# Issuing one small store of the output from SyncE instead of GpSimd, at the end of a gated attention and convolution kernel

## The chip, the cores and the metric

One core of a Trainium2 chip. The kernel is one program with an instruction stream for each engine: TensorE (PE, matmuls), VectorE (DVE), ScalarE (ACT), GpSimd (POOL) and SyncE (SP). DMAs are started by instructions in the streams of SP, ACT and POOL and are carried out by the core's 16 DMA engines. The metric is the device time of one execution in microseconds (us), median of several runs.

## The reference

Two branches over a sequence of 2048 rows and 448 columns, mixed by a gate for each row:

```python
def reference(A_x, A_wq, A_wk, A_wv, A_wo, B_u, B_A_re, ..., B_log_dt, B_Dskip, gate_w):
    def _A_ref(x, wq, wk, wv, wo):        # attention: 16 heads of 28, one key and value head
        q = (x @ wq).reshape(B, S, H, Dh).transpose(0, 2, 1, 3)
        k = x @ wk
        v = x @ wv
        scores = jnp.einsum("bhqd,bkd->bhqk", q, k) * (Dh ** -0.5)
        p = _softmax(scores, axis=-1)
        o = jnp.einsum("bhqk,bkd->bhqd", p, v)
        return o.transpose(0, 2, 1, 3).reshape(B, S, H * Dh) @ wo
    def _B_ref(u, A_re, A_im, B_re, B_im, C_re, C_im, log_dt, Dskip):
...
        P = jnp.exp(logdA[:, :, None] * l[None, None, :])
        K = jnp.einsum("dn,dnl,dn->dl", Cc, P, dB).real      # one filter of 2048 taps for each column
...
        return y + u * Dskip[None, None, :]                  # y: each column of u convolved with its filter
    g = _sigmoid((x * gate_w).sum(-1, keepdims=True))
    return g * a + (1 - g) * b
```

Inputs and output are bf16; the output has 1 x 2048 x 448 elements.

## The kernel before

**The output in SBUF.** The tile `O` has 128 partitions and 16 blocks of 448 columns. Partition p of block t holds row 1024 * (p // 64) + 64 * t + p % 64, so one block is 64 rows of the first half of the sequence and 64 of the second. A store from `O` to the output is therefore always a pair of DMAs, one for each half (`rows`, L1272).

**Who writes `O`.** The convolution goes by chunks of 16 columns, 28 of them (`conv`, 0 to 27): matmuls (L1155) of filter against input, a multiplication by 1 - g (L1170, tile `cst`), a transposition on PE (L1181), and an addition into `O` on DVE (L1189), which touches the chunk's 16 columns in all 16 blocks. So the last 32 columns of every block are complete only with chunks 26 and 27, the last two. The attention branch goes by query blocks; for each block of rows the output projection (L1198, and L1265 for the last one) is multiplied by the gate and added into `O` on DVE (`fold`, L1207). The two kinds of additions commute, and the kernel keeps two keys for each part of the rows: `O` for columns 0 to 415, and `Oz` for the last 32.

**How the output leaves.** All in `tail` (L1250):

- `out0` to `out3` (L1276): columns 0 to 415 of blocks 0 to 14, four pairs of DMAs on SP, which need `O` alone.
- `outz0` and `outz1` (L1282): the last 32 columns, pieces of 64 bytes. `outz0` holds blocks 0 to 7 (m = 8, 512 pieces for each of the two DMAs), `outz1` blocks 8 to 14 (m = 7, 448 pieces for each). Each needs the additions of chunks 26 and 27, and those of the attention for its rows. `outz0` is issued by POOL, `outz1` by ACT.
- `outl0` and `outl1` (L1285): block 15 with all its columns, one DMA each, 64 pieces of 896 bytes, issued by SP and by ACT.

The `outz` and `outl` stores wait for the addition of chunk 27 (L1189), the `out` stores do not.

**What sets the order.** The kernel builds a list of operations with their dependences (`op`, `dma`) and a planner (`schedule`, L178) sets the order on each engine. It simulates the engines: of all operations that are ready it takes the one with the smallest key (time at which it can start, priority `pr`, place in the list), over all engines, and puts it at the end of its engine's stream. The stores all have priority 1. `emit` (L400) then writes each engine's stream in that order, each operation with its waits on semaphores; a DMA adds 16 to the semaphore of its name when it has landed. A stream runs in order: an operation that waits holds up all behind it on its engine. At the end of its stream SP waits for all semaphores whose names begin with `out` (L430 and L431).

**The end of the program.** The streams stand in a block (`with nc.Block() as block`, L483). When its stream ends, each engine drains, and then the engines wait for each other on two semaphores; POOL collects the arrivals and lets the others go. In the profile these instructions carry line 483.

Of the kernel before, what the change touches and what calls it, by code (L numbers as in the profile page):

```python
# [75 lines left out]
def dram(t, off, dims):  # L76
    return bass.AP(tensor=t.tensor, offset=t.offset + off, ap=[list(d) for d in dims])
# [381 lines left out]
class Kernel:  # L459
# [790 lines left out]
    def tail(self):  # L1250
        pg = self.pg
        self.norm_last(14, 0, 512, None, [("on", 2)])
        self.norm_last(15, 0, 256, None, [("on", 3)])
        for tt in range(2):
            self.outp(3, tt)
        self.norm_last(15, 256, 128, None, [("on", 4)])
        self.outp(3, 2)
        self.evac(15, 384, 128)
        self.norm_last(15, 384, 128, 1, [("on", 5)])
        t, o = self.bank(2)  # L1260
        px = lambda: t.v(0, P, o, [[1, D]])
        X, key = ("ox", 3, 3), [("b", 2)]
        on = [("on", 0), ("on", 1), ("on", 2), ("on", 5)]
        for g in range(4):
            pg.op("pe", lambda e, g=g: e.matmul(  # L1265
                px(), self.onT.v(0, P, g * 512 + 384, [[1, 128]]), self.Wo.v(0, P, g * D, [[1, D]]),
                start=(g == 0), stop=(g == 3), tile_position=(0, 0), skip_group_check=True), 200,
                rd=["Wo", on[g]], wr=[X] + key, pr=1 if g < 3 else 0.5)
        self.fold(3, 3, px, 0, D, [X])
        D0 = D - 32  # L1270
        n0 = len(pg.ops)
        rows = lambda t0, m, d0, n: [(dram(self.out, (1024 * h + 64 * t0) * D + d0, [[D, 64], [64 * D, m], [1, n]]),  # L1272
                                      self.O.v(64 * h, 64, D * t0 + d0, [[D, m], [1, n]])) for h in range(2)]
        for qc in range(4):
            m = 4 if qc < 3 else 3
            pg.dma(rows(4 * qc, m, 0, D0),  # L1276
                   (128 * m, 832), f"out{qc}", rd=[("O", q) for q in ([qc], range(3, 6))[qc == 3]], pr=1)
        for i in range(n0, len(pg.ops)):
            pg.after[i] = self.lastT
        for k, e in enumerate(("pool", "act")):  # L1280
            m = 8 - k
            pg.dma(rows(8 * k, m, D0, 32),  # L1282
                   (128 * m, 64), f"outz{k}", rd=[("Oz", q) for q in (range(2), range(2, 6))[k]], pr=1, eng=e)
        for h, e in enumerate(("sp", "act")):
            pg.dma(rows(15, 1, 0, D)[h:h + 1], (64, 896), f"outl{h}", rd=[("O", 6), ("Oz", 6)], pr=1, eng=e)  # L1285
# [193 lines left out]
```

## Time and profile before

| | |
|---|---|
| median of 3 runs | 511.47 us (511.31 to 512.3) |
| the profiled execution | 510.55 us |
| its span in the profile | 508.8 us |
| mean granted TensorE clock | 0.978 |
| busy: PE, DVE, ACT, POOL | 429.2, 454.5, 481.6, 167.0 us |
| last exponential on ACT ends | 493.85 us |
| last addition into `O` on DVE ends | 499.34 us |
| stores of the output issued | 475.9 to 501.5 us |

Times in the profile are counted from the start of its span, in us; the span begins with the first instruction of the program and ends with its last, and the time of an execution is a little longer. A name like L1189 is a line of the kernel. An engine's name with a q (POOLq, SPq) stands for its instruction stream: DMA issues on SP and ACT, waits, drains. A line such as "A <- B" in a list of waits says that A stood idle until B was done; where several things were waited for, the one that came last by the profile is named. The chain is followed backwards from the last busy instruction, and issuing a DMA on POOL counts as busy, while drains and semaphores do not.

In the 40 slices of the span, ACT is 90% busy or more from the fifth slice to the 36th; the last slice, from 496.1 us on, holds the last matmuls, the last additions and the stores:

```profile
PE   6798778888888898889888899989888899998891
...
DVE  7999899999999999999999999999999999624152
ACT  5997999999999999999999999999999999998970
POOL 8632224152152510515422421535151324240001
```

### The profile page before, as it was taken

Reading aid. Unit: us, or ns where it says so; the run is one execution under the profiler, and the core shown is the slowest. Engines: PE = TensorE matmul, PEld = TensorE weight load, DVE = VectorE, ACT = ScalarE, POOL = GpSimd, SP = SyncE. Lnnn points to the kernel's source line nnn. Section 1 sums busy time; section 2 is a strip of 40 time slices with the busy share of each in tenths; the row PEclk is TensorE's granted clock in tenths of the full one; section 3 lists DMA queues with packets and bytes.
Section 4 is the critical chain, followed back from the end, with each engine's and each line's share of the span. In section 5 each row is a group of like instructions: output and inputs, shape, how many; then the busy total and the mean of one; then the engine's idle time right before and its main releaser. Section 6 shows DMA issues by size and latency. Waiting matters only on the chain.

```text
span 508.8 us, 18819 instructions
## 1 busy us (share of the span) xinstructions
PE 429.2 (84%) x8362; PEld 195.4 (38%) x8469; DVE 454.5 (89%) x834; ACT 481.6 (95%) x432; POOL 167.0 (33%) x310
## 2 busy tenths in 40 slices
PE   6798778888888898889888899989888899998891
PEld 2322223343334334344443344444433444344551
DVE  7999899999999999999999999999999999624152
ACT  5997999999999999999999999999999999998970
POOL 8632224152152510515422421535151324240001
PEclk8997999999999999999999999999999999998996
DMA  8979702989959897999999999599999989899932
GB/s 189 220 209 136 51 22 60 331 243 366 359 149 320 260 295 244 299 367 345 348 316 367 306 364 358 150 351 363 363 301 372 312 297 366 266 379 371 385 119 46
DMA packets 122404, 139.51 MB, mean 274 GB/s; under 512 B 55145, under 2 KB 62346, under 8 KB 122322
## 3 DMA queue, kind: packets, MB, share of 16 engines
q1 hardware_dynamic: 111152, 128.82, 79.3%
q0 software_dynamic: 8720, 9.31, 6.7%
q8 instruction: 66, 1.08, 0.9%
q10 hardware_dynamic: 2450, 0.17, 0.3%
q14 instruction: 16, 0.13, 0.1%
HBM read 125.18 MB, written 5.22 MB: 256 GB/s over the span
## 4 chain that ended last, share of the span: by engine, by line
ACT 52%; DVE 36%; PE 8%; issue 2%; DMA 1%; SPq 1%; POOL 0%
ACT expT L1357 52%; DVE tab L1048 4%; DVE tab L1060 3%; DVE tab L1059 3%; DVE msq L991 2%; DVE tab L1070 2%; DVE tab L1058 2%; DVE tab L1057 2%; DVE mbf L1011 2%; PE psS L1332 1%; DVE T L888 1%; DVE seedz L995 1%; PE psB L1383 1%; DVE seedz L993 1%; DVE tmp L1066 1%
## 5 line engine op out<-in xcount | busy, mean ns | idle before, releaser
L1357 ACT ACTIVATE expT<-psS 128x1536 bf16<-128x1536 f32 (+1 forms) x410 | 465.4, 1336 | 6.4 <-PE psS L1323 3.5
L1332 PE MATMUL psS<-qM,kT 128*128 128x512 bf16 (+2 forms) x369 | 104.0, 357 | 28.4 <-ACT expT L1357 14.5
L1383 PE MATMUL psB<-expT,vaug 128*32 128x512 bf16 (+2 forms) x1152 | 102.9, 367 | 2.5 <-issue 1.1
L1323 PE MATMUL psS<-qT,kT 29*128 29x512 bf16 (+2 forms) x699 | 82.4, 363 | 23.4 <-ACT expT L1357 21.5
L154 POOL DMA_DIRECT2D KP_scratch<-kstg x112 | 61.0, 553 | 66.3 <-DVE kstg L1110 37.9
L1048 DVE TENSOR_TENSOR tab<-tab,mbf 128x512 bf16<-128x512 bf16 (+3 forms) x56 | 64.5, 1153 | 0.0
L1383 PEld LDWEIGHTS psB<-expT,vaug 128*32 128x32 bf16 x1152 | 27.5, 93 | 75.4 <-issue 70.4
L154 POOL DMA_DIRECT2D rdenB<-R_scratch x56 | 28.9, 522 | 60.7 <-DMA R_scratch<-denT 51.9
L1332 PEld LDWEIGHTS psS<-qM,kT 128*128 128x128 bf16 x455 | 28.6, 98 | 48.7 <-ACT expT L1357 33.4
L1323 PEld LDWEIGHTS psS<-qT,kT 29*128 29x128 bf16 x699 | 21.3, 91 | 67.3 <-ACT expT L1357 55.7
L154 POOL DMA_DIRECT2D qM<-qT x64 | 32.2, 511 | 35.4 <-DVE qT L966 20.0
L1060 DVE TENSOR_TENSOR tab<-tab 128x128 bf16<-128x128 bf16 (+4 forms) x70 | 41.5, 594 | 0.0
L1059 DVE TENSOR_TENSOR tab<-tab 128x1024 bf16<-128x1024 bf16 (+4 forms) x70 | 41.4, 593 | 0.0
L1155 PE MATMUL psS<-T,U 128*32 128x128 bf16 (+3 forms) x1504 | 35.7, 222 | 0.5 <-DVE qT L966 0.4
L154 POOL DMA_DIRECT2D denT<-acc x14 | 10.0, 715 | 75.5 <-DVE kstg L1106 37.3
L1070 DVE TENSOR_TENSOR tab<-tab,tmp 128x4096 bf16<-128x4096 bf16 x14 | 32.0, 2287 | 0.1
L1058 DVE TENSOR_TENSOR tab<-tab,mbf 128x4096 bf16<-128x4096 bf16 x14 | 31.9, 2279 | 0.0
L1057 DVE TENSOR_TENSOR tab<-tab,mbf 128x4096 bf16<-128x4096 bf16 x14 | 31.9, 2278 | 0.0
L1155 PEld LDWEIGHTS psS<-T,U 128*32 128x32 bf16 (+3 forms) x1504 | 25.3, 95 | 14.2 <-issue 9.9
L1155 PE MATMUL psX<-T,U 128*32 128x128 bf16 (+7 forms) x1216 | 28.8, 220 | 0.4 <-issue 0.2
L991 DVE TENSOR_TENSOR msq<-seedz 128x384 f32<-128x384 f32 (+1 forms) x50 | 27.0, 540 | 0.2
L1066 DVE TENSOR_TENSOR tmp<-tmp,mq 128x64 bf16<-128x64 bf16 (+4 forms) x70 | 25.4, 362 | 0.1
(161 smaller groups left out, 536.8 us busy)
## 6 DMA issues: line engine op xcount, KB each, us to landing
T<-KP_scratch SPq DMA_DIRECT2D x170, 512.0 KB, 9.4
U<-KP_scratch SPq DMA_DIRECT2D x40, 512.0 KB, 10.0
tab<-KP_scratch SPq DMA_DIRECT2D x14, 512.0 KB, 10.6
rdenB<-R_scratch POOLq DMA_DIRECT2D x56, 64.0 KB, 5.5
qM<-qT POOLq DMA_DIRECT2D x64, 32.0 KB, 5.2
tab<-in_A_x_dram SPq DMA_DIRECT2D x8, 224.0 KB, 3.6
O<-cst SPq DMA_DIRECT2D x1, 1792.0 KB, 11.5
KP_scratch<-kstg POOLq DMA_DIRECT2D x112, 16.0 KB, 4.1
```

What stands on the lines that cost most here:

```text
L154: return [e.dma_start(o, i, **kw) for o, i in pairs]
L1048: vo(lambda e, dst=dst, src=src, mri=mri: e.tensor_tensor(dst, src, mri, ALU.mult), 4 * n, done + mk(lv), [kr, ki, tk])
L1057: vo(lambda e, src=src, mi=mi, tv=tv: e.tensor_tensor(tv, src, mi, ALU.mult), 2 * n, done + mk(lv), [tk])
L1058: vo(lambda e, dst=dst, src=src, mr=mr: e.tensor_tensor(dst, src, mr, ALU.mult), 2 * n, done + mk(lv), [kr, ki, ("gap", s)])
L1059: vo(lambda e, dc=dc, tc=tc: e.tensor_tensor(dc[0], dc[0], tc[1], ALU.subtract), n, [tk, kr], [kr])
L1060: vo(lambda e, dc=dc, tc=tc: e.tensor_tensor(dc[1], dc[1], tc[0], ALU.add), n, [tk, ki], [ki])
L1070: vo(lambda e: e.tensor_tensor(tab.v(0, P, FM, [[4, 1024], [1, 4]]), tab.v(0, P, lo + 124, [[CG, 32], [-4, 32], [1, 4]]), rho.v(0, P, 0, [ ...
L1155: r = e.matmul(ps.v(32 * j, 32 - 2 * n, 128 * k, [[1, 128]]), self.U.v(0, P, (4 * gi + j) * 32 + 2 * n, [[1, 32 - 2 * n]]), tbuf.v(0, P, t ...
L1323: r = e.matmul(self.psS.v(0, P, 512 * b + o, [[1, n]]), kT.v(32 * h, DH + 1, 128 * kt, [[1, 128]]), qT.v(32 * h, DH + 1, 512 * (i % 2) + q ...
L1332: r = e.matmul(self.psS.v(0, P, 512 * b + o, [[1, n]]), kT.v(0, P, 128 * kt, [[1, 128]]), self.qM.v(0, P, (i % 2) * XQ + 512 * h + qo, [[1 ...
L1357: pg.op("act", lambda e: e.activation(expT.v(0, P, 512 * es[0], spread(es, n)), self.psS.v(0, P, 512 * bs[0], spread(bs, n)), AF.Exp, scal ...
L1383: r = e.matmul(self.psB.v(32 * h, 32, qo, [[1, n]]), vaug.v(0, P, 32 * kt, [[1, 32]]), expT.v(0, P, 512 * ring[t] + o, [[1, n]]), start=(k ...
```

## The change

The engine of `outz0` is SyncE instead of GpSimd. Its two DMAs, their addresses and sizes, what they depend on, their priority and their place in the list stay. `outz1` stays on ACT.

```diff
--- before.py
+++ after.py
@@ -1277,7 +1277,7 @@
                    (128 * m, 832), f"out{qc}", rd=[("O", q) for q in ([qc], range(3, 6))[qc == 3]], pr=1)
         for i in range(n0, len(pg.ops)):
             pg.after[i] = self.lastT
-        for k, e in enumerate(("pool", "act")):
+        for k, e in enumerate(("sp", "act")):
             m = 8 - k
             pg.dma(rows(8 * k, m, D0, 32),
                    (128 * m, 64), f"outz{k}", rd=[("Oz", q) for q in (range(2), range(2, 6))[k]], pr=1, eng=e)
```

## The prediction

> **What bounds the kernel now.** I read the page first (span, slices, chain shares), then the chain in order of time for the last 14 us, then the end of the program, line 483, then the stores one by one.
>
> ```profile
> span 508.8 us, 18819 instructions
> ...
> ACT 52%; DVE 36%; PE 8%; issue 2%; DMA 1%; SPq 1%; POOL 0%
> ```
>
> Until 493.85 us the last exponential on ACT ends the chain (its timeline row: 487.39 + 6.46), and nothing of that stretch is touched. The chain in order of time shows what follows; columns are start, duration, what.
>
> ```profile
> 497.59 0.69 DVE cst L1170
> ...
> 498.91 0.43 DVE O L1189
> 499.34 0.28 issue
> 499.62 1.44 POOL out_dram L154 x2
> ```
>
> DVE's last addition into O, of convolution 27, ends at 499.34. It releases every store that holds the last 32 columns. The chain ends with POOL's second issue at 499.62 + 1.44 = 501.06, but the span ends at 508.8: 7.7 us have no busy instruction at all. What stands there is seen at line 483, the end of the program's block, where each engine drains and then meets the others (columns: durations in ns, minimum/median/maximum, then first and last start in us):
>
> ```profile
> L483 POOLq EVENT_SEMAPHORE  x2: 17/17/17, 508.6 to 508.7; - x2
> ...
> L483 DVEq DRAIN  x1: 441/441/441, 498.9 to 498.9; - x1
> L483 POOLq DRAIN  x1: 8215/8215/8215, 500.4 to 500.4; - x1
> L483 ACTq DRAIN  x1: 401/401/401, 501.6 to 501.6; - x1
> ...
> L483 SPq DRAIN  x1: 13/13/13, 503.9 to 503.9; - x1
> L483 SPq EVENT_SEMAPHORE  x1: 17/17/17, 508.7 to 508.7; - x1
> ```
>
> Read it by who comes last. PE, DVE and ACT are drained by 502.0. SP, which waits for all stores, is drained at 503.9. POOL's drain starts at 500.4, lasts 8.215 us and ends at 508.6, and only then do the event semaphores of all engines pass, 0.2 us before the span ends. The waits of SP's queue say the same from the other side: 3.7 us for the stores to land, then 4.8 us at line 483 (the engine named there, PE, was long done; POOL's drain is the one still open).
>
> ```profile
> SPq L483 <- PEq L483: 4.8, 1, 4.8
> SPq L431 <- DMA out_dram<-O: 3.7, 2, 3.5
> ```
>
> So the end is set by POOL's drain behind its last two DMAs, by 508.6 - 503.9 = 4.7 us over SP.
>
> **The change part by part.**
>
> Removed from POOL: two DMA issues. POOL's timeline shows what is then its last work:
>
> ```profile
> 453.34 2.00 POOL L154 DMA_DIRECT2D rdenB<-R_scratch  x4 [1.08 <-DVE onT L1225]
> 499.62 1.44 POOL L154 DMA_DIRECT2D out_dram<-O  x2 [44.28 <-DVE O L1189]
> ```
>
> Its instructions end at 455.34, so its drain comes 44 us earlier. How long a drain is there the trace does not show; the bounds are the 183 ns of POOL's drain at line 1464, at the start, before any DMA of its own, and the 8.2 us above. I take 8.2, as it too stands behind POOL DMAs: it ends at about 463.5. Either costs nothing, since ACT works until 493.85, DVE until 499.34 and the stores until 503.7; it would count only from over 48 us on. With that cover gone it is the 4.7 us of today.
>
> Added to SP: the same two DMAs (512 pieces of 64 bytes each). SP has nothing between the rest of `out3` (issued from 495.88) and its `outl0` at 499.36, for which it waited 2.2 us on the same DVE addition. Both are ready at that point, of one priority, and `outz0` comes first in the list, so I expect `outz0`, `outz0`, `outl0`. SP is moved past nothing else: behind `outl0` stands only its wait for all stores. The trace has these rows for stores of the output (columns as above):
>
> ```profile
> L154 SPq DMA_DIRECT2D out_dram<-O x9: 493/1215/1538, 475.9 to 499.4; - x9
> L154 ACTq DMA_DIRECT2D out_dram<-O x3: 656/704/735, 499.4 to 500.9; - x3
> L154 POOL DMA_DIRECT2D out_dram<-O x2: 714/726/738, 499.6 to 500.4; - x2
> ```
>
> and among the DMA issues from 455 us on, with size and median us from issue to landing:
>
> ```profile
> out_dram<-O POOLq DMA_DIRECT2D x2, 32.0 KB, 3.0
> out_dram<-O SPq DMA_DIRECT2D x1, 56.0 KB, 1.9
> out_dram<-O ACTq DMA_DIRECT2D x2, 28.0 KB, 2.8
> out_dram<-O ACTq DMA_DIRECT2D x1, 56.0 KB, 2.8
> ```
>
> One issue of 512 small pieces on SP is not in the trace. Bounds: 0.49 us (SP's `outl0`) and 0.84 (ACT's 0.735 for 448 such pieces, times 8/7); I take 0.74, about ACT's longest, and with 0.03 us between issues, as ACT has. Then `outl0` is issued at 499.36 + 2 x 0.77 = 500.90 instead of 499.36. For its landing the bounds are 1.9 (its own now) and 3.2 (the slower of ACT's two 28 KB stores); I take 2.8, that of ACT's `outl1`, which like it stands third behind two small-piece stores. It lands at 503.7. ACT's `outl1`, untouched, is issued at 500.86 and also lands at 503.7, today's last landing. The 16 DMA engines have as much to move as before, and are no more than 0.62 busy in any stretch from 500 on (the windows by stage).
>
> The sum: last landing 503.7, as today; SP's last waits, branch and drain 0.25 behind it, as today (503.96 is the drain's end); release of the barrier 0.2, as between POOL's drain and the span's end, and 0.1 for SP's signal to reach POOL, an estimate from the less than 0.1 between the event semaphores there. 503.96 + 0.04 + 0.2 + 0.1 = 504.3 against 508.8, a gain of 4.5 us. The profiled execution took 510.55 with 1.75 outside the span, which I leave as it is, and lies 0.9 below the median of the runs; on that median 511.47 - 4.5 = **507.0 us**.
>
> Its own range: landing 2.3 (ACT's first small store) instead of 2.8, should POOL's packets no longer be in the way of either queue, gains 0.5 more; issues of 0.84 and a landing of 3.2 lose 0.6; the runs before spread over 1.0. That is 506.0 to 508.2.
>
> **The rivals.**
>
> One generator for both hardware queues. If SP's and ACT's issues could not overlap, six would follow each other from 499.36: 2 x 0.74, 0.704, 0.735, 0.656, 0.49 and gaps, 4.2 us together, so the last is issued near 502.95 and lands at 505.8, 2.1 later. Gain 2.4, **509.0 us**. For it: at 499.36, where SP and ACT issue at the same moment, ACT's issue took no less than its later ones, so nothing excludes a wait inside it. Against it: from 0.81 to 3.59 SP made four issues in 2.78 us, its usual 0.6 to 0.8 each, while ACT made its own from 0.81 on without a break. Chance 0.10. [...]
>
> The drain does not follow POOL's last DMA but the end of all work. Then it would outlast the last landing as now, by 4.9 us, and the time stays at **511.5 us**. For it: POOL's issues were done at 501.06 and its data had landed at 503.5, yet the drain ran 5.1 us longer, so it waits for something else than these. Against it: SP's and ACT's drains end without any such tail, and at 39.5 us a POOL copy starts right as the DMA before it ends, so DMAs leave nothing behind on POOL that every later step must wait for. Chance 0.13. That the store lands no sooner is granted already: the gain comes from the drain alone.
>
> The other side: SP is held up at its issue. SP's longest issue in this kernel is 5.56 us (one of the four loads of `Wo` from 33.2 on), where its queue had much in front. Should both small-piece stores be held so, `outl0` comes 2 x (5.56 - 0.74) = 9.6 us later, the end at 513.9, and the time is **516.6 us**, slower. It decides from the point where the two issues together take over 1.5 + 4.5 = 6.0 us. For it: `outz0` and `outl0` would share one queue, and SP's issues while its queue was full (475.9 to 483.3) took 1.2 to 1.5. Against it: `out3` has landed by then but for its last pieces, and ACT issues the same kind in 0.70 to 0.735. Chance 0.07.
>
> That the change does not do what it says comes to an order: with `outl0` ahead of `outz0`, the second `outz0` is issued at 500.66 and lands at 503.9 with the 3.2 of ACT's second, 507.2 us, inside the forecast's range.
>
> **How the numbers follow.** Forecast 0.70, shared generator 0.10, drain at the end 0.13, held-up SP 0.07. A difference under 0.2% (1.0 us) can hardly be told from none here. Faster: 0.70 + 0.10 = 0.80; within: 0.13; slower: 0.07. The range takes in the forecast's own and the shared generator with a little beside: 505.9 to 509.3; the two cases outside make 0.20.
>
> **What would show it.** In the changed kernel's line 483, POOL's drain starts near 455 and SP's is the last, near 504; SP's wait at line 483 falls from 4.8 to some tenths. Line 154 has three SP issues from 499.36 on, of 0.5 to 0.84 each, and no POOL store. Landings of `outl0` and `outl1` near 503.7. The prediction is wrong if POOL's drain still ends 4 us or more behind the last landing, if the SP issues overlap ACT's only in turn (over 1.4 us each), or if the exponentials end later than 493.9, which nothing here should move.

## The result and the profile after

The changed kernel takes 507.12 us (median of 6 runs, 505.02 to 507.33), the kernel before 511.39 (6 runs, 510.78 to 512.3): a ratio of 0.9909, 95% interval 0.989 to 0.9927, or 4.3 us less. In a later comparison it was 506.97 (5 runs) against 512.09 (11 runs), 0.9902, 0.9878 to 0.9926.

Line 483 of the changed kernel, the end of the program's block (durations in ns minimum/median/maximum, then first and last start in us):

```profile
L483 POOLq EVENT_SEMAPHORE  x2: 17/17/17, 504.8 to 505.2; - x2
L483 POOLq DRAIN  x1: 10101/10101/10101, 457.0 to 457.0; - x1
...
L483 DVEq DRAIN  x1: 441/441/441, 500.4 to 500.4; - x1
L483 ACTq DRAIN  x1: 404/404/404, 503.1 to 503.1; - x1
...
L483 SPq DRAIN  x1: 13/13/13, 504.8 to 504.8; - x1
```

POOL's drain now runs from 457.0 to 467.1, while ACT is still at its exponentials. SP is the last to drain, and POOL's event semaphores follow, at 504.8 and 505.2. The waits of SP's queue show the same: 4.8 us at line 483 have become 0.5, and the wait for the stores has fallen from 3.7 to 1.5, as SP is busy issuing from 500.86 to 502.81.

```profile
SPq L431 <- DMA out_dram<-O: 1.5, 2, 0.8
SPq L483 <- PEq L483: 0.5, 1, 0.5
```

The stores of the output (issues at line 154, and for those from the last addition on, size and us to landing):

```profile
L154 SPq DMA_DIRECT2D out_dram<-O x11: 596/637/1582, 478.4 to 502.2; - x11
L154 ACTq DMA_DIRECT2D out_dram<-O x3: 662/720/787, 500.9 to 502.4; - x3
```

```profile
out_dram<-O SPq DMA_DIRECT2D x2, 32.0 KB, 2.2
out_dram<-O ACTq DMA_DIRECT2D x2, 28.0 KB, 2.4
out_dram<-O SPq DMA_DIRECT2D x1, 56.0 KB, 2.1
out_dram<-O ACTq DMA_DIRECT2D x1, 56.0 KB, 2.1
```

The last piece of the chain in this profile is DVE's addition:

```profile
499.09 0.69 DVE cst L1170
499.78 0.60 DVE O L1207
500.38 0.02 issue
500.41 0.42 DVE O L1189
```

It stands 1.5 us later than before (500.83 against 499.34), so the spans, 505.3 and 508.8, differ by 3.5 only. I don't put that shift down to the change: a second profile of the same kernel has the last addition at 503.92, and eleven profiles of kernels whose streams are the same up to POOL's last load have the last exponential ending between 492.7 and 498.4. What the change touches is the stretch behind that addition. I call it the tail, and it repeats to hundredths: **9.48 us before, 4.45 and 4.46 in the two profiles after**. That is 5.0 us less; the medians give 4.3 to 5.1.

### The profile page after: what moved, and what is told of

It is laid out like the page before. It is cut to its first block, busy times and chain, and to the rows that moved or that the text cites. A ratio compares the mean times of both kernels' runs of the same rounds, so it can differ in the third digit from the quotient of the medians.

```text
span 505.3 us, 18926 instructions
## 1 busy us (share of the span) xinstructions
PE 448.2 (89%) x8469; PEld 195.1 (39%) x8469; DVE 455.0 (90%) x834; ACT 482.6 (96%) x432; POOL 165.3 (33%) x308
## 3 DMA queue, kind: packets, MB, share of 16 engines
q0 software_dynamic: 8656, 9.25, 6.7%
## 4 chain that ended last, share of the span: by engine, by line
ACT 48%; DVE 38%; PE 10%; issue 2%; DMA 1%; SPq 1%
ACT expT L1357 48%; DVE tab L1048 5%; DVE tab L1059 3%; DVE tab L1060 3%; DVE msq L991 3%; DVE tab L1070 2%; DVE tab L1058 2%; DVE tab L1057 2%; DVE mbf L1011 2%; PE psS L1332 2%; PE psB L1383 2%; DVE seedz L995 2%; PE psS L1323 2%; DVE seedz L993 1%; DVE tmp L1066 1%
## 5 line engine op out<-in xcount | busy, mean ns | idle before, releaser
L1332 PE MATMUL psS<-qM,kT 128*128 128x512 bf16 (+2 forms) x455 | 122.5, 360 | 13.8 <-ACT expT L1357 10.5
```

The costliest lines, as they stand in the source:

```text
L1332: r = e.matmul(self.psS.v(0, P, 512 * b + o, [[1, n]]), kT.v(0, P, 128 * kt, [[1, 128]]), self.qM.v(0, P, (i % 2) * XQ + 512 * h + qo, [[1 ...
```

## The experiments

All are the changed kernel with one edit, but for three small ones at the end. The table holds what the traces gave, in us behind the end of the last addition into `O` (negative: ahead of it). "POOL ends" is the end of POOL's last instruction ahead of its drain.

| kernel | POOL ends | POOL's drain ends | SP's drain ends | tail |
|---|---|---|---|---|
| before | 1.74 | 9.25 | 4.63 | 9.48 |
| after | -43.1 | -33.7 | 3.95 | 4.45 |
| after_again | -44.1 | -34.3 | 3.95 | 4.46 |
| tiny_end | 0.79 | 8.22 | 5.27 | 8.74 |
| memset_end | 0.17 | 7.54 | 3.95 | 8.06 |
| tiny_mid | -2.70 | 4.74 | 3.94 | 5.26 |
| tiny_early | -10.8 | -3.4 | 3.96 | 4.17 |
| memset_early | -11.4 | -4.1 | 3.96 | 4.18 |
| memset_461 | -37.6 | -30.3 | 3.97 | 4.19 |
| on_act | -44.3 | -34.5 | 5.58 | 6.09 |
| halves | -44.1 | -34.2 | 3.94 | 4.43 |

**A late DMA on POOL, but a tiny one.** All stores stay where the change put them; POOL gets one of 64 bytes to a scratch tensor `Z`.

```diff
+        pg.dma([(dram(self.Z, 0, [[32, 1], [1, 32]]), self.O.v(0, 1, 0 * D + D0, [[1, 32]]))], (1, 64), "outd", rd=[("Oz", q) for q in range(2)], pr=1, eng="pool")
```

> The changed kernel with one more DMA on POOL: a single 64-byte piece of O into a scratch tensor in DRAM, released by the same last addition as outz0, so that POOL again has a DMA at its very end, but a tiny one, while all stores of the output stay on SP and ACT. Theory drain (the gain is that POOL's drain of 8 to 10 us no longer stands behind a late DMA): the drain starts some 0.5 us behind the last addition into O and ends 8.8 to 10.5 us behind it; the tail from that addition to the end of the span goes from 4.45 back to 9 to 10.7 us, the time from 507.1 to about 511.6 to 513.3. Rival landing (the gain is that 64 KB land sooner through a hardware queue): tail 4.5 to 5.0, time 507.1 to 507.6. Rival size (the drain is long because 1024 pieces went through POOL): drain well under 4 us, time about 507.1.

Measured: 510.18 us (10 runs) against 511.35, ratio 0.9978, 0.9954 to 1.0002. The tail is 8.74. POOL's timeline and line 483 of this kernel:

```profile
499.97 0.50 POOL L154 DMA_DIRECT2D Z_scratch<-O  x1 [43.43 <-DVE O L1189]
```

```profile
L483 POOLq EVENT_SEMAPHORE  x2: 17/17/17, 508.2 to 508.3; - x2
...
L483 POOLq DRAIN  x1: 7952/7952/7952, 500.0 to 500.0; - x1
...
L483 SPq DRAIN  x1: 13/13/13, 504.9 to 504.9; - x1
```

POOL's drain is last again by 3 us. So it is not the 64 KB, nor where they land, that costs, and a drain behind 64 bytes is as long as one behind 1024 pieces: 7.43 us from the end of POOL's last instruction, 7.51 before. The sizes expected, a tail of 9 to 10.7 us and 511.6 to 513.3 us of time, were too high, since I had counted with the drain of 10.1 us at 457.

The tiny DMA did one thing more in this profile. The six stores behind the addition, issued as in the changed kernel, all took 1.3 to 1.7 us longer to land (that kernel's rows, above, have 2.2, 2.4, 2.1 and 2.1):

```profile
out_dram<-O SPq DMA_DIRECT2D x2, 32.0 KB, 3.7
out_dram<-O ACTq DMA_DIRECT2D x2, 28.0 KB, 4.0
out_dram<-O SPq DMA_DIRECT2D x1, 56.0 KB, 3.4
out_dram<-O ACTq DMA_DIRECT2D x1, 56.0 KB, 3.4
```

So the last landing is at 5.02 instead of 3.70, and SP's drain at 5.27. The tail doesn't feel it, as POOL's drain ends later still, at 8.22. The name `outd` makes SP wait for the tiny DMA too, but that landed at 501.63, before any of the six.

**The same DMA earlier.** It is released by the addition of block 12 (`rd=[("O", 3)]`), with columns of that block as its source.

> The same tiny DMA on POOL, released by the gated addition of block 12 into O instead (about 11.6 us ahead of the last addition). Theory drain: the drain starts there and is over 1.5 to 3 us ahead of the last addition, so the tail stays at 4.45 us and the time at 507.1, within 0.5. Rival that one more POOL DMA costs by itself, wherever it stands: tail 9 us, 511.6.

Measured: 506.24 us (4 runs) against 511.35, 0.9898, 0.9853 to 0.9943. The drain is as long, and hidden:

```profile
L483 POOLq DRAIN  x1: 7952/7952/7952, 487.8 to 487.8; - x1
...
L483 SPq DRAIN  x1: 13/13/13, 503.1 to 503.1; - x1
```

**No late DMA at all, only a late end of POOL's stream.**

```diff
+        pg.op("pool", lambda e: e.memset(self.denT.v(0, P, 0, [[1, 16]]), 0.0), 100, rd=[("Oz", q) for q in range(2)], wr=["dn"], pr=1)
```

> The changed kernel with a small memset on POOL (16 columns of denT, not used afterwards) released by the last additions, so that POOL's stream ends late, with no DMA of POOL for 40 us before. Theory drain (it is POOL's recent DMAs that keep the drain busy): the drain takes under 1 us, the tail stays 4.45 to 4.7, the time 507.1 to 507.4. Rival end of stream (the drain costs 8 to 10 us whenever POOL's stream ends, once it has issued DMAs at all): drain 8 us or more, tail 9 to 10.5, time 511.6 to 513.

My theory fell here. Measured: 511.28 us (10 runs) against 511.35, ratio 0.9985, 0.9959 to 1.0011: the time can't be told from the kernel before. By the tail, 8.06 us, 3.6 of the 5.0 us gained are gone again. Timeline and line 483:

```profile
498.25 0.11 POOL L1283 MEMSET denT<- 128x16 f32 x1 [43.21 <-DVE O L1189]
```

```profile
L483 POOLq EVENT_SEMAPHORE  x2: 17/17/17, 506.1 to 506.1; - x2
...
L483 POOLq DRAIN  x1: 7497/7497/7497, 498.2 to 498.2; - x1
...
L483 SPq DRAIN  x1: 13/13/13, 502.1 to 502.1; - x1
```

POOL's last DMA had landed 37 us earlier, all stores are on SP and ACT, and the drain still takes 7.37 us behind a memset of 0.11. So it is not the late DMA that keeps the drain busy. It is the late end of POOL's stream, in all three kernels whose stream ends behind the last addition: 7.51 us behind the stores, 7.43 behind the tiny DMA, 7.37 behind the memset. The other theory on record named this, with a drain of 8 us or more, which was a little too long. The same memset near 462 and 489 us (memset_461 and memset_early, below) has the same 7.37 us behind it, so the length doesn't come from what else goes on at the end.

**From where on it counts.** The tiny DMA released by the addition of block 14 (`rd=[("O", 5)]`).

> The tiny DMA on POOL released by the gated addition of block 14, 3.5 us ahead of the last addition. Theory now (POOL's last drain takes 7.4 to 7.5 us from the end of POOL's last instruction, whatever that is): POOL's DMA issue ends 2.6 to 2.8 us ahead of the end of the last addition, the drain ends 4.6 to 4.9 behind it, where SP's own drain stood at 3.9: the barrier waits for POOL by 0.7 to 1.0, tail 4.9 to 5.2 us instead of 4.45. If the drain counted from the landing of all stores, tail 8 us or more.

Measured in the one profile: POOL ends 2.70 ahead of the end of the last addition, its drain 4.74 behind, the tail is 5.26, and one run took 508.64. The expected sizes hold; the tail is 0.06 over the range given. So with SP's drain at 3.95, POOL's last instruction has to end at least 7.4 - 3.95 = 3.5 us ahead of the last addition, or it sets the end.

**The store on ACT instead of SP.** `enumerate(("act", "act"))`.

> outz0 on ACT instead of SP, so ACT issues five stores and SP one. Theory drain: POOL's drain stays early, near 457, and the gain stays but for a later last landing: outl1 is issued fifth, 4 x 0.75 = 3.0 us behind the first instead of 1.5, so the tail is 4.45 + 1.5 = 6.0 us and the time 508.6, still 2.8 faster than before. Rival that SP's queue as such is what gains: the time goes back to 511 or more.

Measured: 509.11 us (10 runs) against 511.35, 0.9948, 0.9919 to 0.9976; the tail is 6.09. ACT's queue:

```profile
500.57 3.67 ACTq L154 DMA_DIRECT2D out_dram<-O  x5
```

Leaving POOL brings the gain, and a third of it is lost again where five issues stand in one queue: the last landing is at 5.27 behind the addition instead of 3.70. So SP is worth 1.6 us over ACT, by sharing out the issues.

**Fewer issues.** The small stores cut by halves, 960 pieces each on SP and ACT:

```diff
+        for h, e in enumerate(("sp", "act")):
+            pg.dma(rows(0, 15, D0, 32)[h:h + 1],
+                   (64 * 15, 64), f"outz{h}", rd=[("Oz", q) for q in range(6)], pr=1, eng=e)
```

> The two small-piece stores cut by halves of the sequence instead of by blocks: SP stores the last 32 columns of blocks 0 to 14 for the first half (960 pieces, one DMA), ACT the same for the second half, then each its outl. Each queue issues two DMAs at the end instead of three. With POOL's drain out of the way, the tail is the third issue and its landing: if the number of issues sets it, the last issue starts 0.75 us behind the first instead of 1.3 to 1.6, the tail falls from 4.45 to 3.7 to 4.1 us, the time by 0.4 to 0.8 us under the changed kernel. Rival that the 1920 small pieces themselves set the landing: tail 4.4 to 4.5, no change.

A miss: 507.58 us (6 runs) against 512.09, 0.9918, 0.9893 to 0.9943, and a tail of 4.43. The issues did come earlier, the last at 501.69 with the addition at 500.90, but the landings took longer by as much:

```profile
out_dram<-O SPq DMA_DIRECT2D x1, 60.0 KB, 2.6
out_dram<-O ACTq DMA_DIRECT2D x1, 60.0 KB, 3.3
out_dram<-O SPq DMA_DIRECT2D x1, 56.0 KB, 2.9
out_dram<-O ACTq DMA_DIRECT2D x1, 56.0 KB, 2.9
```

With the same 1920 small pieces on the way the last landing stays at 3.68, so in the changed kernel the number of issues doesn't set it, while five issues on one queue, above, do. That the pieces set it fits both kernels, but no run has fewer of them.

**The changed kernel again.**

> The changed kernel again, on the same chip as halves. Tail 4.45 us (within 0.3), time 4.3 us under before; the time of the last exponential may differ by 1 to 2 us from the first profile, if that shift has nothing to do with the change.

Its time and tail are given above; the profiled execution took 510.18 us, with the last exponential 3.0 us later than in the first profile and a mean clock of 0.977 against 0.985.

**What makes the drain long.** Two small kernels that compute nothing of the reference:

> A small kernel by itself that computes nothing of the reference: DVE fills a tile 16 times, SP stores it as the output, POOL does one small memset at the start and one behind DVE's last fill, and issues no DMA at all. If a late drain of POOL costs 7.4 us whatever POOL has done before: a drain of 7.4 to 7.5 us behind the memset. If it takes an earlier DMA issued by POOL: under 0.5 us.

> The small kernel that computes nothing of the reference, with one DMA on POOL (128 pieces of 128 bytes to a scratch tensor) at the start, landed some 55 us before POOL's last memset. If an earlier DMA issued by POOL is what makes its last drain long: 7.4 us behind the memset, against the 0.2 us of the kernel without it. If the large kernel's drain is long for another reason (its many instructions, its hundreds of POOL DMAs): under 0.5 us.

Their last drains are 226 and 322 ns, 0.07 and 0.16 us behind the memset. So a drain without any DMA of POOL before is short, and one DMA adds some 0.1 us, not 7. That left a count, which a third small kernel tested with five blocks in a row:

> A small kernel that computes nothing of the reference (it stores a filled tile as output): five blocks one after the other, each ending with a memset on POOL and a drain; before the memset POOL issues 0, 32, 128, 32 and 0 DMAs of its own and waits for them (the first 32 and the 128 have 128 pieces of 128 bytes, the second 32 have 512 pieces of 64 bytes). Drain behind the memset with no DMA of POOL: 0.07 us (one run), with one: 0.16, in the large kernel with 266: 7.37. Theory count (the drain takes 0.027 us for each DMA that POOL has issued since its last drain): 0.07, 0.95, 3.6, 0.95, 0.07 us behind the memsets. If it counts all DMAs since the start: 0.07, 0.95, 4.4, 5.3, 5.3. If it goes by pieces and not by DMAs: the fourth is four times the second. If the large kernel's 7.4 us have another cause: all under 0.5.

The five drains in the order of the blocks (line 25 is each block's end):

```profile
L25 POOLq DRAIN  x1: 47/47/47, 1.7 to 1.7; - x1
```

```profile
L25 POOLq DRAIN  x1: 2676/2676/2676, 39.0 to 39.0; - x1
```

```profile
L25 POOLq DRAIN  x1: 1267/1267/1267, 136.9 to 136.9; - x1
```

```profile
L25 POOLq DRAIN  x1: 123/123/123, 169.4 to 169.4; - x1
```

```profile
L25 POOLq DRAIN  x1: 46/46/46, 170.1 to 170.1; - x1
```

Neither count as expected fits: 32 DMAs 2.68 us, 128 only 1.27, 32 larger ones 0.12, none 0.05. The timeline tells more. In the third block POOL stands still for 2.81 us, waiting for nothing that the profile shows, ahead of its last 15 DMAs, and in the fourth for 2.10 ahead of its last one.

```profile
122.52 0.54 POOL L42 DMA_DIRECT2D Z_scratch<-W  x1 [1.46 <-DMA Z_scratch<-W]
125.86 3.73 POOL L42 DMA_DIRECT2D Z_scratch<-W  x7 [2.81 <-issue]
131.04 4.26 POOL L42 DMA_DIRECT2D Z_scratch<-W  x8 [1.46 <-DMA Z_scratch<-W]
136.52 0.15 POOL L45 MEMSET V<- 128x64 bf16 x1 [1.22 <-DMA Z_scratch<-W]
```

Counted from there it is 2.68 / 32 = 0.084, 1.27 / 15 = 0.084 and (0.123 - 0.046) / 1 = 0.08 us for each DMA. My estimate, from these three drains alone, is that the drain finishes something for every DMA that POOL has issued since it last did so, in a drain or in such a stall. In the large kernel the drain grows in step: 7.37 us with 266 DMAs of POOL, 7.43 with 267, 7.51 with 268. But there 7.4 / 0.084 is 88 DMAs, while 138 to 140 followed a stall of that kind of 2.3 us near 249 us. A second one, of 1.5 to 1.7 us near 409 us, is followed by 35 to 37, which would make 3 us. Neither fits. What is finished, and how many of the 266 still count at the end, stays open.

**POOL's two semaphores.** In the changed kernel POOL's two event semaphores at the end stand 0.37 us apart, before 0.08, and in the kernels with one POOL instruction more 0.08 again.

> The changed kernel with a memset on POOL behind the landing of its last load (near 461 us), so that POOL's stream has one instruction more but still stands idle for over 30 us at the end. Drain 7.4 to 10 us from about 461, hidden; tail within 0.1 of 4.45 us if POOL's long idleness is what makes its two event semaphores at the end stand 0.37 us apart, 4.17 if it is the place of the instructions in the stream.

> The changed kernel with a memset on POOL released by the gated addition of block 12, near 488 us. Its drain ends near 495.5, before the last addition, and costs nothing; POOL's two event semaphores at the end stand 0.08 us apart instead of 0.37, as with the tiny DMA there, so the tail is 4.17 us, 0.28 under the changed kernel; the time is about 507 or 0.3 less, which the runs can't tell from it.

memset_461: tail 4.19, with POOL idle from 469.6 to 503.8, so it is not the idleness. memset_early: 506.86 us (4 runs) against 512.77, 0.9876, 0.9819 to 0.9933, tail 4.18. With one instruction more in POOL's stream, near 462 (memset_461), 488 (tiny_early) or 489 us (memset_early), the tail is 0.26 to 0.28 us shorter (4.19, 4.17 and 4.18 against 4.45); why, no run shows. By time it can't be told from the changed kernel, and nothing tried here beats that by more.

## Why the prediction was right

Forecast 507.0 us, measured 507.12. Point by point:

- **The end is set by POOL's drain.** Shown: memset_end and tiny_end bring the late drain back and with it most of the tail (8.06 and 8.74 of 9.48 us), with all stores on SP and ACT. "POOL's drain behind its last two DMAs" named the right instruction with too narrow a cause: a memset in place of the DMAs has nearly the same drain behind it (7.37 us against 7.51). The change gains because POOL's stream ends at 457.8 and no longer at 501.1.
- **A drain moved to 455 is hidden.** Right. It took 10.1 us there instead of the 8.2 taken, with 34 us to spare. POOL's last load landed only at 463.41, and the drain ended 3.69 us behind that, as it did in each of the four kernels of the last section.
- **Order and issues on SP.** The order is as expected. The issues took 0.60, 0.64 and 0.64 us; I had taken 0.74, 0.74 and 0.49. `outl0` started 1.32 us behind the first one, not 1.54.
- **Landing.** The mis-sized term: 2.8 us for `outl0`, where 2.1 were measured, and ACT's untouched `outl1` fell from 2.8 to 2.1 too, so the last landing is 3.70 behind the addition instead of 4.38. The range's lower end had a reason for this, "should POOL's packets no longer be in the way", and tiny_end speaks for it: with one late DMA on POOL, of 64 bytes, the same landing took 3.4 us. It is one profile, and in tiny_mid, where POOL's DMA was issued 3.2 us ahead of the addition's end, the landings are as in the changed kernel. Before, two instruction fetches of 8 KB also fall among the stores, after it one, at their end; in tiny_end the only one starts at 504.35, when the first store had landed 1.5 us late already, so these are not needed for it.
- **Barrier** (the engines' wait for each other at the end). 0.50 us from SP's drain to the end, where I took 0.3: the gap between POOL's two semaphores is 0.29 us wider than before. This takes back 0.2 of the 0.7 that the landing gave: the tail was forecast at 504.3 - 499.34 = 5.0 and is 4.45. The 0.04 in the sum has no row behind it; without it the sum is 504.26, the same to a tenth. The upper end of the forecast's own range, by its own terms, is 508.1 and not 508.2.
- **A sign that failed.** The prediction calls itself wrong if the exponentials end later than 493.9. They ended at 495.41. But over the eleven profiles named above their end lies anywhere from 492.7 to 498.4, so this sign can't tell the change from that scatter.
- **The rivals.** A shared generator: SP's three issues (500.86 to 502.81) and ACT's three (500.86 to 503.09) run side by side, and in on_act ACT issued its last three stores with no issue of SP beside them, in 0.66, 0.65 and 0.51 us; beside SP the same three took 0.72, 0.79 and 0.66, so a wait for each other is at most 0.15 us an issue and not a turn of 0.6. These rows show no turns of whole issues; a shorter wait inside an issue they don't exclude. The drain at the end of all work: ruled out, it was over at 467 with stores still to come. SP held up at its issue: no issue from 500 on took over 0.64.

That the time was met to 0.1 us is partly luck: the gain in the tail was 5.0 against the 4.5 forecast, and the medians of each set carry half a microsecond or more of what happens ahead of it.

## What to carry to other kernels

In these kernels the end of the program is the last engine to drain (POOL at 508.6 before, SP at 504.8 after), not the last busy instruction (501.06 and 500.83): read the drains at the end of the block before any transfer. An engine whose drain is long has to end its stream early, here POOL by 3.5 us ahead of the last addition, and the late instructions tried on it, a DMA of 64 bytes and even a memset of 0.1 us, cost most of what the late store did (tails of 8.74 and 8.06 us against 9.48). And compare a change at the end by the stretch behind a fixed instruction: here it repeated to 0.01 us while the span moved by 3.

## What the runs showed of the hardware that was not expected

- POOL's drain is long without recent DMAs: 7.37 us behind a memset, more than 40 us behind POOL's last DMA issue; 0.07 us in a program in which POOL issues none. In a small kernel (drains) it was 0.08 us for each DMA issued since the last drain or stall: 2.68 us for 32, 1.27 for 15.
- Where POOL's last DMA landed late, the drain ended late too. In the four kernels where it landed 5.6 to 6.1 us behind the end of POOL's last instruction (after, after_again, on_act and halves) the drain ran 9.3 to 9.8 us from there, and ended 3.69 us behind the landing in every one. That is half of the 7.37 us that it takes when all has landed; why is open.
- With one DMA of 64 bytes issued on POOL 0.3 us behind the addition the landings of six stores on SP and ACT took 1.3 to 1.7 us longer (tiny_end, one profile).
- The last of 1920 pieces of 64 bytes and the stores behind them landed 3.7 us behind the addition, whether they came in six issues or in four.
